# Attention and two gated layers on one core: another order for the first scores, their PSUM banks and the preparation of head pairs 1 and 2

## The chip, the cores and the metric

The kernel runs on one core of one Trainium2 chip. The metric is the device time of one execution in microseconds (us); lower is better. Before the change the median of three runs is 707.9 us (707.78 to 710.27).

## What is computed

Sixteen attention heads (2 batches of 8, 1152 positions, 64 columns) whose queries are averaged over pairs of positions, so that each head has 576 query rows against 1152 keys; then two gated layers on the 1152 by 512 result.

```python
q_pool = q.reshape(B, H, S // 2, 2, D).mean(axis=3)
scores = q_pool @ k.T / sqrt(D);  scores -= max(scores)
attn = exp(scores) / (sum(exp(scores)) + 1e-9);  o = attn @ v
x = o as (1152, 512)
xn = x / sqrt(mean(x*x) + 1e-6) * rms_g
x = (silu(xn @ w_gate) * (xn @ w_val)) @ w_out
out = (sigmoid(x @ w_gate2) * (x @ w_val2)) @ w_out2
```

## The kernel before, in words

The 16 heads are taken as 8 **pairs**; the two heads of a pair sit on partitions 0 to 63 and 64 to 127, so that two products of 64 rows run side by side on TensorE (PE). A pair's 576 query rows are cut into **chunks**: 1 to 4 of 128 rows, and chunk 0 with the last 64 rows of both heads. All products keep almost full precision: a tensor is split into a high part and a low part (`kh`, `kl` for keys, the two halves of `q` for queries), and each score is a sum of three products.

The work of a pair has these steps, and each has its helper:

- Raw Q, K and V come by DMA, issued by SyncE (SP) in program order (`load_q`, `load_k`, `load_v`, lines 307 to 327). GpSimd (POOL) adds the two positions of each query pair (`pool_q`, L333). It can only do so when raw Q has landed.
- PE turns pooled Q and raw K around (transposes, all of them on line 295, into tiles `qT` and `kT`), ScalarE (ACT) copies them out of PSUM (L359 to `kqt`) and POOL splits them (`prep_step` and `split`, L133 and L134). For pair 0 `prep_first` (L376 to L446) does this in pieces: K in three thirds, Q in chunks 1 and 2 first and 3, 4 and 0 later. There ACT writes the high part (L418), and VectorE (DVE, L421) or POOL (L425, from an ACT copy on L424) the low part.
- A **score unit** (`s_unit`, L448) is one chunk against one third of the keys (u = 0, 1, 2: 384 columns) for both heads: six matmuls of 384 columns on L467, into two PSUM banks with the tag "s", of which there are three. DVE takes the unit out of PSUM with its row maximum (`top`, L472, one per head; after the third unit of a chunk a small L474). Chunk 0 has its own three units on L464.
- When a chunk has all three units, ACT takes the exponentials (`expo`, L478, tile `e`).
- PE transposes the exponentials (`t_units`, tile `eT`, 24 or 30 of them on L295 in each cycle), into one of two double banks with the tag "t" that `qT` and `kT` use as well; ACT and DVE copy them to `et`.
- PE multiplies them by V (`av_unit`, L528, tile `o`, which has one bank of its own, tag "o"). Later steps turn the result into `x` and feed the gated layers (L683, L793, L822).

The order on each engine is written out by hand. An agenda (`at`, `run_agenda`, L119) holds steps with a slot g and a rank, and issues them in that order; each engine then runs its own queue in order and waits on semaphores. Eight slots are a cycle and six cycles are a pair (48 slots). `S_UNITS` says in which cycle and at which place of it a pair's units of chunks 1 to 4 stand, counted from the pair's first cycle; a cycle has two of them, and a pair's units begin five cycles ahead. `S_UNITS_SECOND` is pair 1's own table, which has three units in two of its cycles (cycles 3 and 4 of the program). `PREP` gives the cycles in which the next pair's Q, first five ninths of K and last four ninths of K are turned. Pair 0's first units start at slot -37.

The two lines that the units rest on are these:

```python
s = [bank("s", "s")[:, 0:SU] for j in heads]
for n, (x, ks) in enumerate(((0, kh), (0, kl), (1, kh))):
```

Of the kernel before, what the change touches and what calls it, by code (L numbers as in the profile page):

```python
# [27 lines left out]
S_UNITS_SECOND = ((-4, 1, 1, 0), (-3, 0, 1, 1), (-3, 1, 1, 2), (-3, 2, 2, 0), (-2, 0, 2, 1), (-2, 1, 2, 2), (-2, 2, 3, 0)) + S_UNITS[7:]  # L28
# [5 lines left out]
PREP = ((0, 1, 2), (-3, -2, 0))  # L34
# [17 lines left out]
def tile_attention_moe_moe(ctx, tc, q, k, v, w_gate1, w_val1, w_out1, rms_g, w_gate2, w_val2, w_out2, out):  # L52
# [315 lines left out]
    def prep_pair(c0, p):  # L368
        alloc_pair(p)
        slots = [(c0 + x) * CYCLE + PREP_SUB for x in PREP[p > 1]]  # L370
        at(slots[0], 1, lambda: prep_step(slots[0], q_group(p, (1, 2, 3, 4, 0), raw['s', p])))
# [4 lines left out]
    def prep_first():  # L376
# [64 lines left out]
        def turn():  # L441
            step(g0 + CYCLE + 1, q_group(0, (3, 4, 0), qs), True)

        at(g0 + 2, 21, rest)
# [423 lines left out]
```

## Time and profile before

| what | us |
|---|---|
| median of three runs | 707.9 |
| the profiled execution, its own time | 708.78 |
| its span, first to last instruction | 707.0 |
| PE busy in the span | 681.2 |
| DVE busy | 399.7 |
| ACT busy | 379.7 |
| POOL busy | 294.1 |

The span is what the profile shows of an execution; the execution's own time is 1.8 us more. Times in the rows are counted from the start of the span. The attention ends at about 253 us; the gated layers follow. PE counts as busy from the start of a matmul to its modelled end.

### The profile page before, as it was taken

How to read it: one execution, taken by the hardware profiler on the slowest of the kernel's cores; microseconds unless marked ns; L12 is line 12 of the kernel's file. 1: busy time of each engine (PE TensorE's matmuls, PEld its weight loads, DVE VectorE, ACT ScalarE, POOL GpSimd, SP SyncE). 2: the span in 40 equal slices, each digit the busy share in tenths (PEclk: the TensorE clock that was granted, in tenths of full speed). 3: DMA queues.
4: the chain of work that ended last, by engine and by line, in shares of the span. 5: the costliest groups of instructions: out<-in, count | busy, mean ns of one | idle time of the engine just before them, and what ended most of it. 6: DMA issues, size and time to landing. Idle time of an engine off the chain costs nothing.

```text
span 707.0 us, 13681 instructions
## 1 busy us (share of the span) xinstructions
PE 681.2 (96%) x5420; PEld 603.9 (85%) x5420; DVE 399.7 (57%) x1020; ACT 379.7 (54%) x708; POOL 294.1 (42%) x280
## 2 busy tenths in 40 slices
PE   7989999998989789999999999999999999999997
PEld 5767777776666489999999999999999999998886
DVE  4777887886886456886676533332546544642010
ACT  3768798797876436655454453324454545544000
POOL 3533364457431105663354374414434534537000
PEclk9999999999999999999999999999999999999999
DMA  6323314313111003332331243213113222222011
GB/s 183 112 69 107 93 47 134 97 42 96 34 33 32 2 0 116 118 124 62 90 116 64 68 142 116 69 32 112 60 61 119 67 84 90 90 69 80 1 74 59
DMA packets 66783, 55.92 MB, mean 79 GB/s; under 512 B 20896, under 2 KB 61856, under 8 KB 66720
## 3 DMA queue, kind: packets, MB, share of 16 engines
q1 hardware_dynamic: 66720, 55.06, 25.7%
q8 instruction: 42, 0.69, 0.4%
q14 instruction: 21, 0.17, 0.1%
HBM read 52.69 MB, written 2.36 MB: 78 GB/s over the span
## 4 chain that ended last, share of the span: by engine, by line
PE 64%; DVE 0%; issue 0%
PE acc L683 42%; PE acc L793 11%; PE acc L822 10%; PE xT L610 0%; DVE xa L599 0%; DVE ob L832 0%
## 5 line engine op out<-in xcount | busy, mean ns | idle before, releaser
L683 PE MATMUL acc<-xh,w 128*128 128x384 f32 (+2 forms) x1184 | 296.4, 331 | 0.0
L683 PEld LDWEIGHTS acc<-xh,w 128*128 128x128 f32 x1184 | 212.7, 189 | 0.1
L683 PE MATMUL acc<-xl,w 128*128 128x384 f32 (+2 forms) x592 | 196.0, 331 | 0.0
L244 POOL TENSOR_TENSOR w<-wr,w 128x512 fp32r<-128x512 f32 x68 | 100.0, 1471 | 186.8 <-ACT w L243 169.3
L472 DVE TENSOR_SCALAR_CACHE_REDUCE e<-s 128x384 f32<-128x384 f32 x216 | 114.3, 552 | 41.1 <-PE s L467 29.9
L229 POOL TENSOR_TENSOR wr<-wsg,wr 128x512 uint32<-128x512 uint32 x72 | 93.7, 1301 | 50.8 <-DVE wsg L223 43.5
L683 PEld LDWEIGHTS acc<-xl,w 128*128 128x128 f32 x592 | 111.6, 189 | 0.0
L478 ACT ACTIVATE e<-e,m 128x1152 f32<-128x1152 f32 x72 | 90.7, 1261 | 5.7 <-DVE m L474 5.7
L467 PE MATMUL s<-kh,q 64*128 64x384 f32 x384 | 87.0, 400 | 6.0 <-DVE e L472 5.1
L694 ACT ACTIVATE sg<-acc 128x384 f32<-128x384 f32 (+2 forms) x74 | 35.7, 482 | 104.3 <-PE acc L683 104.2
L697 DVE TENSOR_TENSOR sg<-acc,sg 128x384 f32<-128x384 f32 (+2 forms) x74 | 40.5, 547 | 84.6 <-PE acc L683 78.5
L528 PE MATMUL o<-et,vraw 128*64 128x320 f32 (+1 forms) x576 | 81.1, 418 | 0.0
L223 DVE SCALAR_TENSOR_TENSOR wsg<-wg,wsg 128x512 uint32<-128x512 uint32 x72 | 77.0, 1069 | 2.3
L201 ACT ACTIVATE wg<-wraw 128x512 f32<-128x512 f32 x72 | 48.4, 673 | 47.7 <-DVE wsg L223 38.7
L793 PE MATMUL acc<-hh,w 128*128 128x384 f32 x288 | 73.2, 334 | 0.0
L528 PEld LDWEIGHTS o<-et,vraw 128*64 128x64 f32 x576 | 37.5, 138 | 30.7 <-issue 10.1
L514 ACT ACTIVATE et<-eT 128x512 f32<-128x512 f32 x96 | 52.0, 598 | 21.1 <-PE eT L295 20.5
L467 PEld LDWEIGHTS s<-kh,q 64*128 64x128 f32 x384 | 50.8, 202 | 14.5 <-DVE e L472 11.9
L219 DVE TENSOR_SCALAR wsg<-wg 128x512 uint32<-128x512 uint32 x72 | 41.3, 573 | 35.0 <-POOL wr L229 34.9
L295 PE MATMUL eT<-ident,e 64*128 64x64 f32 x1296 | 54.3, 226 | 5.3 <-DVE xl L629 3.7
L295 PEld LDWEIGHTS eT<-ident,e 64*128 64x128 f32 x1296 | 51.4, 141 | 9.2 <-DVE xl L629 4.4
L208 ACT ACTIVATE wr<-wraw 128x512 uint32<-128x512 uint32 x72 | 47.9, 666 | 9.5 <-POOL w L244 8.5
(97 smaller groups left out, 872.7 us busy)
## 6 DMA issues: line engine op xcount, KB each, us to landing
wraw<-in_moe_w_gate_dram SPq DMA_DIRECT2D x24, 512.0 KB, 3.5
wraw<-in_moe_w_val_dram SPq DMA_DIRECT2D x24, 512.0 KB, 3.5
wraw<-in_moe_w_out_dram SPq DMA_DIRECT2D x24, 512.0 KB, 3.5
vraw<-in_v_dram SPq DMA_DIRECT2D x16, 288.0 KB, 3.1
kraw<-in_k_dram SPq DMA_DIRECT2D x14, 288.0 KB, 4.7
qraw<-in_q_dram SPq DMA_DIRECT2D x14, 256.0 KB, 3.7
out_dram<-ob SPq DMA_DIRECT2D x9, 256.0 KB, 2.0
qraw<-in_q_dram SPq DMA_DIRECT2D x14, 64.0 KB, 3.7
```

Of the source, the lines that this page charges most:

```text
L223: nc.vector.scalar_tensor_tensor(x["s"], x["g"], 3, x["s"], op0=ALU.logical_shift_left, op1=ALU.bitwise_or)
L229: nc.gpsimd.tensor_tensor(x["r"], x["s"], x["r"], op=ALU.add)
L244: nc.gpsimd.tensor_tensor(t[:, 1], r, t[:, 0].bitcast(F32), op=ALU.subtract)
L295: nc.tensor.transpose(t[:, j, (x0 + x) * 64:(x0 + x + 1) * 64], rows[j][r, cols], ident[r, r])
L467: nc.tensor.matmul(s[j], qt[r, x, QOF[c]:QOF[c] + P], ks[r, kc], start=(n == 0), stop=(n == 2))
L472: nc.vector.tensor_scalar(etile[p, c, j][:, kc], s[j], 1.0, None, op0=ALU.mult, op1=ALU.max, accum_out=m[:, u:u + 1])
L478: nc.scalar.activation(e, e, AF.Exp, bias=emin[p, c, j][:, NSU:NSU + 1], scale=1.0, accum_out=both_sums[p][:, j, c:c + 1])
L514: op = nc.vector.tensor_copy if n in E_DVE[cyc % NCYC] else lambda d, x: nc.scalar.activation(d, x, AF.Copy)
L528: nc.tensor.matmul(o[r, 0:n], vsb[p][:, j, kc], et[:, j * n:(j + 1) * n], start=(kc == 0), stop=(kc == NK - 1))
L683: nc.tensor.matmul(acc[:, 0:nt], wt[:, ws, dc * P:(dc + 1) * P], xs[:, dc], start=(dc == 0 and n == 0), stop=(dc == NDM - 1 and n == 2))
L793: nc.tensor.matmul(acc[t][:, 0:NTT], w[:, ws, (fc % 4) * P:(fc % 4 + 1) * P], hs[fc][:, cs], start=(fc == 0 and n == 0), stop=(fc == NFC - ...
L822: nc.tensor.matmul(acc[r][:, 0:DM], hs[fc][:, r * P:(r + 1) * P], w[:, ws, :], start=(fc == 0 and n == 0), stop=(fc == NFC - 1 and n == 2))
```

## The change

- In every score unit the three products come as high key by high query, high key by low query, low key by high query; the low part of K is used last, not second.
- Pair 0's first nine units get a table of their own (`S_FIRST`, slots -11 to -1): the first thirds of chunks 1 and 2 come first, and each third of K is turned just ahead of the units that use it. Every other unit takes one "s" bank and the "o" bank instead of two "s" banks. The rest of the table, chunk 4 and chunk 0, keeps its slots.
- Pair 1's Q and the first part of its K are turned at slot 0, ahead of the unit at slot 0, and the rest of its K at slot 8 (before: 0, 8 and 16). Pair 2's are turned at 40, 48 and 56 (before: 24, 32 and 48). Pair 1's units start one cycle sooner, and no cycle has three of them. `pool_q` of pair 1 moves from slot -8 to -5 of the new count, that of pair 2 from 16 to 32.
- SP issues raw Q and K of pair 1 ahead of V of pair 0.

```diff
-S_UNITS_SECOND = ((-4, 1, 1, 0), (-3, 0, 1, 1), (-3, 1, 1, 2), (-3, 2, 2, 0), (-2, 0, 2, 1), (-2, 1, 2, 2), (-2, 2, 3, 0)) + S_UNITS[7:]
+S_UNITS_SECOND = ((-5, 1, 1, 0), (-4, 0, 2, 0), (-4, 1, 1, 1), (-3, 0, 1, 2), (-3, 1, 2, 1)) + S_UNITS[5:]
+FIRST = -12
+S_FIRST = ((1, 1, 0), (3, 2, 0), (4, 1, 1), (5, 1, 2), (6, 2, 1), (7, 2, 2), (9, 3, 0), (10, 3, 1), (11, 3, 2))
-PREP = ((0, 1, 2), (-3, -2, 0))
+PREP_SLOTS = (-3, -2, 0)
+PREP = ((0, 0, 8), (5 * CYCLE, 6 * CYCLE, 7 * CYCLE))
...
-        slots = [(c0 + x) * CYCLE + PREP_SUB for x in PREP[p > 1]]
+        slots = PREP[p - 1] if p < 3 else [(c0 + x) * CYCLE + PREP_SUB for x in PREP_SLOTS]
...
+        load_q(1)
+        load_k(1)
         load_v(0)
-        load_k(1)
-        load_q(1)
...
-        for n, g in enumerate((g0 + 1, g0 + 4)):
-            at(g, 3, lambda n=n, g=g: step(g, k_group(0, 3 * n + 3, 3 * n + 6, kr), n == 1))
+        for n, x in enumerate((2, 3)):
+            at(FIRST + x, 3, lambda n=n, g=FIRST + x: step(g, k_group(0, 3 * n + 3, 3 * n + 6, kr), n == 1))
...
-        at(g0 + 2, 21, rest)
-        at(g0 + CYCLE + 1, 3, turn)
-        at(g0 + 2 * CYCLE, 22, lambda: diagonal(0))
+        at(FIRST + 4, 21, rest)
+        at(FIRST + 6, 3, lambda: step(FIRST + 6, q_group(0, (3, 4, 0), qs), True))
+        at(FIRST + 9, 22, lambda: diagonal(0))
...
-    def s_unit(g, p, c, u):
+    def s_unit(g, p, c, u, tags="ss"):
...
-        s = [bank("s", "s")[:, 0:SU] for j in heads]
-        for n, (x, ks) in enumerate(((0, kh), (0, kl), (1, kh))):
+        s = [bank(tags[j], "s")[:, 0:SU] for j in heads]
+        for n, (x, ks) in enumerate(((0, kh), (1, kh), (0, kl))):
...
+        if p == 0:
+            for n, (x, c, u) in enumerate(S_FIRST):
+                at(FIRST + x, 2, lambda g=FIRST + x, c=c, u=u, n=n: s_unit(g, 0, c, u, ("ss", "so")[n % 2]))
+        for x, n, c, u in (S_UNITS[-3:], S_UNITS_SECOND)[p] if p < 2 else S_UNITS:
-            at((cyc0 + min(PREP[p > 0])) * CYCLE, 0, lambda cyc0=cyc0, p=p: prep_pair(cyc0, p + 1))
-            at((cyc0 + POOL_Q) * CYCLE if p else -CYCLE, 50, lambda p=p: pool_q(p + 1))
+            at(min(PREP[p]) if p < 2 else (cyc0 + min(PREP_SLOTS)) * CYCLE, 0, lambda cyc0=cyc0, p=p: prep_pair(cyc0, p + 1))
+            at((-5, 4 * CYCLE)[p] if p < 2 else (cyc0 + POOL_Q) * CYCLE, 50, lambda p=p: pool_q(p + 1))
```

What moves on the engines is read from the order of the two programs' instructions. First PE at its start, behind the first transposes of Q (`kT<-ident,first` turns a third of pair 0's K, `s<-kh,q` and `s<-kl,q` are the products of score units), before:

```order
L295 MATMUL kT<-ident,first 128x64 x6
L467 MATMUL s<-kh,q 128x384 x2
L467 MATMUL s<-kl,q 128x384 x2
L467 MATMUL s<-kh,q 128x384 x2
L295 MATMUL kT<-ident,first 128x64 x12
L467 MATMUL s<-kh,q 128x384 x2
L467 MATMUL s<-kl,q 128x384 x2
L467 MATMUL s<-kh,q 128x384 x4
```

and now:

```order
L298 MATMUL kT<-ident,first 128x64 x6
L466 MATMUL s<-kh,q 128x384 x4
L466 MATMUL s<-kl,q 128x384 x2
L298 MATMUL kT<-ident,first 128x64 x6
L466 MATMUL s<-kh,q 128x384 x4
L466 MATMUL s<-kl,q 128x384 x2
L298 MATMUL kT<-ident,first 128x64 x6
```

The last two thirds of K were turned together behind the first unit; now each stands behind one unit more, and the low part of K closes a unit instead of standing in its middle.

Second, PE where the first exponentials are transposed (`eT<-ident,e`; `qT<-ident,qsum` and `kT<-ident,kraw` turn Q and K of pair 1, and `s<-kh,qbd` begins chunk 0), before:

```order
L467 MATMUL s<-kh,q 128x384 x2
L295 MATMUL qT<-ident,qsum 128x64 x10
L467 MATMUL s<-kh,q 128x384 x2
L467 MATMUL s<-kl,q 128x384 x2
L467 MATMUL s<-kh,q 128x384 x2
L295 MATMUL eT<-ident,e 128x64 x24
```

and now:

```order
L466 MATMUL s<-kl,q 128x384 x2
L298 MATMUL qT<-ident,qsum 128x64 x10
L298 MATMUL kT<-ident,kraw 128x64 x10
L466 MATMUL s<-kh,q 128x384 x4
L466 MATMUL s<-kl,q 128x384 x2
L298 MATMUL eT<-ident,e 128x64 x24
```

Ten transposes of pair 1's K have come ahead of the unit before the first exponentials. In both programs ten score units of pair 0 (chunks 1 to 3 and the first third of chunk 4) stand ahead of the first `eT`.

Third, POOL at the same time (`kl<-kqt,kh` is the low part of the last third of K, `qsum<-first` pools pair 0's Q, `q<-kqt,q` its late low part, `qsum<-qraw` pools pair 1's Q), before:

```order
L414 TENSOR_TENSOR qsum<-first 128x2x64 x3
L414 TENSOR_TENSOR qsum<-first 128x64 x2
L425 TENSOR_TENSOR kl<-kqt,kh 128x384
L425 TENSOR_TENSOR q<-kqt,q 128x384
L366 COPY qbd<-q 64x2x64 x2
L333 TENSOR_TENSOR qsum<-qraw 128x2x5x64
```

and now:

```order
L417 TENSOR_TENSOR qsum<-first 128x2x64
L428 TENSOR_TENSOR kl<-kqt,kh 128x384
L417 TENSOR_TENSOR qsum<-first 128x2x64 x2
L417 TENSOR_TENSOR qsum<-first 128x64 x2
L428 TENSOR_TENSOR q<-kqt,q 128x384
L336 TENSOR_TENSOR qsum<-qraw 128x2x5x64
```

The low part of the last third of K has come ahead of the late sums of Q, and pair 1's pooling ahead of the copies of `qbd`.

## Rows read from the trace of the kernel before

**Rows 1.** The page's first part: busy time, share of the span, instructions.
```profile
PE 681.2 (96%) x5420; PEld 603.9 (85%) x5420; DVE 399.7 (57%) x1020; ACT 379.7 (54%) x708; POOL 294.1 (42%) x280
```
**Rows 2.** Busy time in three stretches: length, engines, granted clock, DMA share, GB/s.
```profile
0.00:24.00 24.00, 17.98 (x105) 13.15 (x107) 12.10 (x48) 9.72 (x17) 7.90 (x20) 1.00 0.69 190
24.00:48.00 24.00, 21.48 (x284) 16.35 (x282) 17.38 (x66) 18.39 (x32) 12.64 (x14) 1.00 0.28 77
48.00:100.00 52.00, 51.85 (x706) 37.84 (x704) 40.51 (x158) 42.02 (x77) 22.95 (x30) 1.00 0.31 83
```
**Rows 3.** Timeline, one turn of the score loop: start, length, engine, [idle before <-releaser].
```profile
17.73 0.56 DVE L472 TENSOR_SCALAR_CACHE_REDUCE e<-s 128x384 f32<-128x384 f32 x1 [0.63 <-PE s L467]
18.21 0.08 DVE L472 DVE_READ_ACCUMULATOR e<-s 128x1 f32 x1
18.33 0.16 DVE L474 TENSOR_REDUCE m<-m 128x1 f32<-128x3 f32 x1
18.35 0.69 PE L467 MATMUL s<-kh,q 64*128 64x384 f32 x1 [0.35 <-DVE e L472]
18.40 0.55 DVE L472 TENSOR_SCALAR_CACHE_REDUCE e<-s 128x384 f32<-128x384 f32 x1
...
19.43 0.56 DVE L472 TENSOR_SCALAR_CACHE_REDUCE e<-s 128x384 f32<-128x384 f32 x1 [0.28 <-PE s L467]
```
**Rows 4.** Timeline of the head: low parts, first maximum, late low part of Q.
```profile
6.94 0.69 PE L467 MATMUL s<-kl,q 64*128 64x384 f32 x2
...
8.83 0.62 DVE L421 SCALAR_TENSOR_TENSOR kl<-kT,kh 128x192 fp32r<-128x192 f32 x2 [1.95 <-ACT kh L418]
...
9.37 0.55 DVE L472 TENSOR_SCALAR_CACHE_REDUCE e<-s 128x384 f32<-128x384 f32 x1
...
10.45 1.01 POOL L425 TENSOR_TENSOR kl<-kqt,kh 128x384 fp32r<-128x384 f32 x1
...
14.29 1.01 POOL L425 TENSOR_TENSOR q<-kqt,q 128x384 fp32r<-128x384 f32 x1 [2.83 <-ACT kqt L424]
```
**Rows 5.** Timeline where the first transposes and the tenth unit's maximum stand.
```profile
24.20 1.48 PE L295 MATMUL eT<-ident,e 64*128 64x64 f32 x21
...
24.55 0.56 DVE L472 TENSOR_SCALAR_CACHE_REDUCE e<-s 128x384 f32<-128x384 f32 x1 [0.35 <-PE s L467]
```
**Rows 6.** Timeline of ACT: the first of the exponentials.
```profile
14.10 1.26 ACT L478 ACTIVATE e<-e,m 128x1152 f32<-128x1152 f32 x1
```
**Rows 7.** Timeline: the first issue behind pair 0's Q, and pair 1's pooling.
```profile
8.44 1.06 SPq L327 DMA_DIRECT2D vraw<-in_v_dram  x2
...
18.51 1.55 POOL L333 TENSOR_TENSOR qsum<-qraw 128x640 f32<-128x640 f32 x1 [2.52 <-DVE m L474]
```
**Rows 8.** DMA issues between 8 and 20 us: count, KB each, median us to landing.
```profile
kraw<-in_k_dram SPq DMA_DIRECT2D x2, 288.0 KB, 4.8
qraw<-in_q_dram SPq DMA_DIRECT2D x2, 256.0 KB, 4.1
```
**Rows 9.** Timeline of PE's waits in pair 0's cycles 2, 3 and 4.
```profile
35.77 0.39 PEld L295 LDWEIGHTS qT<-ident,qsum 64*128 64x128 f32 x10 [0.39 <-POOL kl L134]
...
39.89 0.44 PE L467 MATMUL s<-kh,q 64*128 64x384 f32 x1 [1.09 <-DVE e L472]
...
46.07 0.44 PE L467 MATMUL s<-kh,q 64*128 64x384 f32 x1 [1.09 <-DVE e L472]
```
**Rows 10.** Timeline of PE: chunk 0 of pairs 0, 1 and 2 begins.
```profile
26.72 0.45 PE L464 MATMUL s<-kh,qbd 128*128 128x384 f32 x1
...
56.94 0.44 PE L464 MATMUL s<-kh,qbd 128*128 128x384 f32 x1
...
83.17 0.44 PE L464 MATMUL s<-kh,qbd 128*128 128x384 f32 x1
```
**Rows 11.** Matmuls of one line, 0 to 24 and 60 to 100 us: ns min/median/max.
```profile
L467 PE MATMUL s<-kh,q x39: 518/518/687, 6.3 to 23.9; 64*128 64x384 f32 x39
...
L467 PE MATMUL s<-kh,q x76: 328/376/443, 60.1 to 99.1; 64*128 64x384 f32 x76
```

More of the change, by code (lines that the diff above doesn't have):

```diff
@@ L429, in prep_first @@
             nc.tensor.transpose(warm[:, 0:P], ident, ident)
-        g0 = -4 * CYCLE - 5
         sums(slice(1, 3), (nc.vector, nc.gpsimd))
-        step(g0, q_group(0, (1, 2), qs), False)
-        step(g0, k_group(0, 0, 3, kr), False)
-        for n, g in enumerate((g0 + 1, g0 + 4)):
-            at(g, 3, lambda n=n, g=g: step(g, k_group(0, 3 * n + 3, 3 * n + 6, kr), n == 1))
+        step(FIRST, q_group(0, (1, 2), qs), False)
+        step(FIRST, k_group(0, 0, 3, kr), False)
+        for n, x in enumerate((2, 3)):
+            at(FIRST + x, 3, lambda n=n, g=FIRST + x: step(g, k_group(0, 3 * n + 3, 3 * n + 6, kr), n == 1))
         def rest():
@@ L439, in rest @@
                 sums(c, (nc.gpsimd, nc.gpsimd))
-        def turn():
-            step(g0 + CYCLE + 1, q_group(0, (3, 4, 0), qs), True)
-        at(g0 + 2, 21, rest)
-        at(g0 + CYCLE + 1, 3, turn)
-        at(g0 + 2 * CYCLE, 22, lambda: diagonal(0))
-    def s_unit(g, p, c, u):
+        at(FIRST + 4, 21, rest)
+        at(FIRST + 6, 3, lambda: step(FIRST + 6, q_group(0, (3, 4, 0), qs), True))
+        at(FIRST + 9, 22, lambda: diagonal(0))
+    def s_unit(g, p, c, u, tags="ss"):
         if p not in both_sums:
@@ L484, in s_unit @@
         for n, j in enumerate(heads):
-            at(g + (2 * n if g % CYCLE == S_SUB[0] else 0), 17 + n if c else 10, lambda j=j: top(j))
+            at(g + (2 * n if g % CYCLE == S_SUB[0] and g >= 0 else 0), 17 + n if c else 10, lambda j=j: top(j))
         if u == NSU - 1:
@@ L649, in tile_attention_moe_moe @@
         cyc0 = p * NCYC
-        for x, n, c, u in S_UNITS_SECOND if p == 1 else S_UNITS:
+        if p == 0:
+            for n, (x, c, u) in enumerate(S_FIRST):
+                at(FIRST + x, 2, lambda g=FIRST + x, c=c, u=u, n=n: s_unit(g, 0, c, u, ("ss", "so")[n % 2]))
+        for x, n, c, u in (S_UNITS[-3:], S_UNITS_SECOND)[p] if p < 2 else S_UNITS:
             g = (cyc0 + x) * CYCLE + S_SUB[n]
```

## The prediction

> **What bounds the kernel now.** I read the busy times first. PE is busy 96% of the span, no other engine above 57% [rows 1]. Then three stretches: PE is busy 18.0 of the first 24 us, 21.5 of the next 24 and 51.9 of the 52 behind them [rows 2]. So from 48 us on PE is the bound, and what the change can win lies ahead of that. Chunk 0 of pairs 0, 1 and 2 begins at 26.72, 56.94 and 83.17 [rows 10]: a pair costs 30.22 us the first time and 26.23 the second, when PE has no gap. Whatever is saved ahead of 57 us moves the dense rest to the left whole, since PE's queue is in order and its later work is the same.
>
> In the head the loop of the score units is the bound. A unit takes two of three "s" banks, so the next unit's second head must wait for the first maximum of this one: the maximum starts at 17.73, PE goes on at 18.35 having idled 0.35, and the next unit's maximum starts at 19.43 [rows 3]. From 9.37 to 24.55 there are nine such turns [rows 4, 5]: 15.2 / 9 = 1.69 us each. DVE and PE both idle in each turn.
>
> TensorE's clock matters here. The same matmuls last 518 ns in the head and 328 at the least later [rows 11]. The granted clock reads 1.00 for both stretches [rows 2], but these durations say that the head runs at the lower level, 1.2 GHz, and the rest at 2.4.
>
> **The change, part by part.** An edit with no cost: the new order of the three products has the same six matmuls and weight loads, so beyond the head it is worth 0; PE's density there [rows 2] leaves nothing to hide or lose.
>
> *The pace of the first units.* With "o" as a fourth bank two units are in flight and no unit waits for its neighbour. The bound becomes DVE: a maximum every 0.48 us (17.73 to 18.21), 0.19 more when a reduction follows (18.21 to 18.40) [rows 3]; a chunk is six of the first and two of the second, 3.26 us, so 1.09 per unit. PE is no slower: from its start at 18.35 to the next maximum at 19.43 is 1.08 us, latency included [rows 3].
>
> *The start.* The first unit ended with low queries by high keys; now it ends with the low keys, which PE multiplied from 6.94 for 0.69 us [rows 4], so the first maximum can start at 7.6 instead of 9.37. The 0.62 us of DVE work for the second third's low part [rows 4] stood ahead of it and now stands behind the first unit. The tenth unit's maximum can so start at 7.6 + 0.62 + 9 x 1.09 = 18.0 at the earliest. Before it was 24.55 [rows 5]; the upper end is 6.5 us.
>
> *New waits in the head.* (a) The low part of the last third of K is POOL's, 1.01 us [rows 4], behind ACT's two copies; walking the queues from unit to unit I have it ready at 11.1, and unit 4 then leaves DVE idle 0.6. (b) POOL makes pair 0's late sums of Q behind that and not ahead; their low part, another 1.01 us [rows 4], is ready at 15.0 and unit 7 needs it as its second product: 0.7. (c) Ten transposes of Q and ten of K of pair 1 stand ahead of unit 10. At 1.48 / 21 = 0.07 us [rows 5] they are 1.4, of which some 0.4 lie under DVE's remaining maxima: 1.0. Sum 2.3 us, so unit 10's maximum starts at about 20.3. Bounds: nothing (each input a little sooner) to 4 us (both POOL steps late by one more 1.01, and none of the transposes hidden). I take **4.3 us** won here, with ends of 2.5 and 6.5. ACT is late next: its late copies of Q end at about 13.9, where the four exponentials of 1.26 us [rows 6] begin, and a copy follows, so the first transposes can't start before 19.7; I have them at 20.0 (before 24.20).
>
> *The loads.* Raw Q of pair 1 takes V's place at 8.44 [rows 7]. With four issues of about 0.6 us and 4.1 to land [rows 8] it is there at 15.0, when POOL is free; POOL's 1.55 us end at 16.6 and PE asks at 18. Before it was pooled from 18.51 [rows 7]. Raw K is issued by 12.1 and there at 16.9 [rows 8]. V comes last, by 18.5, for a product at 26. All of it is hidden, with a reserve of over a us.
>
> *K of pair 1.* Ten transposes leave the place behind chunk 0, where the clock is up: half of 0.7 us, so **0.3** back (0 to 0.7).
>
> *Units of pair 1.* Two cycles with three units made PE wait 1.09 us each for a bank, behind DVE [rows 9]. With two units in every cycle, as in the dense pairs, this goes: **2.2 us** (0, if another wait takes its place, to 2.2).
>
> *Q and K of pair 2.* Q's transposes waited 0.39 us for POOL [rows 9]; two cycles later POOL is done: **0.4** (0 to 0.4). In exchange the last part of its K is turned only one cycle ahead of its first use, and a maximum of pair 1 now takes a tile that pair 0's third cycle still reads. Nothing in the trace shows either. They can cost 0, or as much as the nearest waits, 1.09 [rows 9]; each has most of a cycle to hide in, so I take **0.3 lost** for both.
>
> The sum is 4.3 + 0.3 + 2.2 + 0.4 - 0.3 = 6.9 us. A check from the other side: the first pair is 30.22 - 26.23 = 4.0 us longer than the second [rows 10], and the parts outside the head take 2.6 of these. The profiled execution (708.78, span 707.0) so becomes 701.9; it stands 0.9 above the median of 707.9, so the median becomes **701.0 us**.
>
> One rule of the skill speaks against part of this. In the trace the lower clock lasts through the head, and 26.72 already has a chunk-0 matmul of 0.45 us [rows 10]; the stretch before it mixed scores with 21 and more transposes [rows 5]. The Trainium skill (TensorE: Matmul & The Clock Gate, Part 4: PE-mode transpose) says that transposes do not count as PE being busy for the clock. By that rule the twenty transposes now set ahead of unit 10 would hold the clock down longer, and the sum would be the first rival's. No row here separates the two.
>
> **The rivals.**
>
> *The clock stays down until 26 us as before.* It rose at about 26 us, behind a stretch in which PE had no idle time. If it rises no sooner, what is done from 20.0 to 26.3 in the new order runs at 518 where 328 is possible [rows 11]: 6.3 x (1 - 328/518) = 2.3 us, some of it under DVE and ACT, say 2.0: **703.0**. For it: transposes are many there. Against: PE idled 0.35 of each 1.69 [rows 3] and has far less idle time from 8 us on in the new head.
>
> *Only the head gains.* ACT and POOL reach cycles 1 to 4 with less reserve, and new waits take the place of the 2.6 us outside the head: **703.6**. For it: ACT is busy 18.4 of 24 us behind the head [rows 2], and its four exponentials now run without a pause. Against: the later pairs do the same work in 26.2 us without a gap.
>
> *The change doesn't do what it says.* In the order of instructions the first transposes of exponentials stand behind ten units in both programs, so I count nothing for an earlier place. If the fourth bank also fails to quicken the loop, nine turns stay at 1.69: 7.6 + 0.6 + 15.2 = 23.4, a gain of 1.1 in the head and 3.7 in all: **704.2**. Against: the idle time in rows 3 is a wait for a bank and nothing else.
>
> *Slower than before: raw K of pair 1 comes late.* Its transposes now stand in front of unit 10 and of all of pair 0's exponentials, and PE is in order. Each us that K lands behind 18.5 is lost whole, and the gain of 6.9 is gone when it lands behind 25.4. Landing would take 13 us, not 4.8 [rows 8]; at three times 4.8 it is there at 26.5 and the kernel takes **709.0**. For it: the DMA engines are 69% busy in the head [rows 2]. Against: the bytes are the same as before.
>
> **How the numbers follow.** The forecast has a chance of 0.55; its own range, from the ends above, is 699.3 to 702.7. The clock rival has 0.13, the head alone 0.18, the unchanged pace 0.05, the late K 0.05; 0.04 is left for a head at its upper end of 6.5, 698.8. The range 699.0 to 704.6 leaves out the late K, the upper end and the worse third of two rivals, some 0.16. A measurement of this kernel tells about 0.5% from no change, 3.5 us, so faster means below 704.4: nearly all of the forecast (0.54) and the upper end (0.04), most of the clock rival (0.11), a little over half of the head alone (0.10), half of the unchanged pace (0.02): 0.81. Slower by over 0.5% takes a late K beyond its price, 0.03; 0.16 is left.
>
> **What would show it.** Right: unit 10's maximum near 20.3, a loop of about 1.1 us, the first exponentials' transposes at 20, chunk 0 of pair 1 near 50 and of pair 2 26.2 later, and no waits of 1.09 for a bank. The head alone is right if chunk 0 of pair 0 comes over 4 us sooner but that of pair 1 not over 5. The clock rival shows in 518 ns matmuls behind 20 us. The forecast is wrong if the loop stays at 1.69, or if PE waits for `kraw`, for POOL's low parts beyond 1.5 us, or for ACT's exponentials.

## The result, and the profile after

The changed kernel takes 699.89 us, the median of three runs (699.56 to 700.81), against 707.9. The ratio is 0.988 with a 95% interval of 0.985 to 0.991. The forecast was 701.0, so the gain is 8.0 us where 6.9 were expected. The profiled execution of the changed kernel is also 699.89 (span 698.1), against 708.78 (span 707.0).

The busy line of its page, and three windows (columns as in [rows 1, 2]):

```profile
PE 675.8 (97%) x5420; PEld 598.9 (86%) x5420; DVE 399.0 (57%) x1020; ACT 379.8 (54%) x708; POOL 294.0 (42%) x280
```

```profile
0.00:24.00 24.00, 19.09 (x171) 14.36 (x173) 16.01 (x65) 14.38 (x25) 12.00 (x24) 1.00 0.78 213
24.00:48.00 24.00, 23.92 (x328) 16.87 (x325) 18.86 (x74) 19.45 (x35) 9.55 (x14) 1.00 0.22 55
48.00:100.00 52.00, 51.84 (x714) 38.05 (x713) 42.62 (x164) 43.70 (x81) 27.06 (x33) 1.00 0.34 93
```

The second window, where PE was busy 21.48 us [rows 2], is now dense, and DVE does 16.01 us of work in the first one instead of 12.10. Behind 48 us little is different.

DVE's timeline in the head (start, length, engine, line, operation, idle time before it and its releaser): the first maximum, the two places where it then has to wait, and the tenth unit's maximum.

```profile
7.57 0.56 DVE L471 TENSOR_SCALAR_CACHE_REDUCE e<-s 128x384 f32<-128x384 f32 x1 [0.78 <-PE s L466]
...
11.77 0.56 DVE L471 TENSOR_SCALAR_CACHE_REDUCE e<-s 128x384 f32<-128x384 f32 x1 [0.69 <-PE s L466]
...
15.65 0.56 DVE L471 TENSOR_SCALAR_CACHE_REDUCE e<-s 128x384 f32<-128x384 f32 x1 [0.17 <-PE s L466]
...
18.94 0.56 DVE L471 TENSOR_SCALAR_CACHE_REDUCE e<-s 128x384 f32<-128x384 f32 x1
```

Nine turns with a wait in each [rows 3] have become a DVE that works through with 0.86 us of waits in all. The tenth unit's maximum starts at 18.94 instead of 24.55 [rows 5].

PE's timeline: two low-key products of the head, its two waits for POOL from which DVE's come, the first transposes of pair 1, the first of the exponentials, and chunk 0 of pairs 0, 1 and 2.

```profile
8.40 0.53 PE L466 MATMUL s<-kl,q 64*128 64x384 f32 x2
...
9.67 0.34 PE L466 MATMUL s<-kl,q 64*128 64x384 f32 x2
...
11.29 0.45 PE L466 MATMUL s<-kl,q 64*128 64x384 f32 x2 [0.52 <-POOL kl L428]
...
15.00 0.44 PE L466 MATMUL s<-kh,q 64*128 64x384 f32 x2 [0.37 <-POOL q L428]
...
17.21 0.50 PE L298 MATMUL qT<-ident,qsum 64*128 64x64 f32 x8
...
19.45 1.05 PE L298 MATMUL eT<-ident,e 64*128 64x64 f32 x24 [0.48 <-ACT kqt L362]
...
21.01 0.62 PE L463 MATMUL s<-kh,qbd 128*128 128x384 f32 x2
...
47.75 0.62 PE L463 MATMUL s<-kh,qbd 128*128 128x384 f32 x2
...
74.10 0.62 PE L463 MATMUL s<-kh,qbd 128*128 128x384 f32 x2
```

Against [rows 10], chunk 0 of pair 0 begins 5.71 us sooner (21.01 for 26.72), that of pair 1 9.19 sooner, that of pair 2 9.07 sooner, and the span ends 8.9 sooner. So the head won 5.71 and pair 0 another 3.48 (it lasts 26.74 instead of 30.22); from there on the two programs take the same time within 0.3 us. The rows at 8.40 and 9.67 are the same kind of pair of matmuls: 0.53 us, then 0.34. TensorE goes from its lower level (1.2 GHz) to the upper (2.4 GHz) at about 9.5 us. In the kernel before it did so at about 26: its transposes of exponentials at 24.20 are still long [rows 5].

### The profile page after: what moved, and what is told of

The parts are those of the page before. It is cut to its first block, busy times and chain, and to the rows that moved or that the text cites. A ratio compares the mean times of both kernels' runs of the same rounds, so it can differ in the third digit from the quotient of the medians.

```text
span 698.1 us, 13688 instructions
## 1 busy us (share of the span) xinstructions
PE 675.8 (97%) x5420; PEld 598.9 (86%) x5420; DVE 399.0 (57%) x1020; ACT 379.8 (54%) x708; POOL 294.0 (42%) x280
## 4 chain that ended last, share of the span: by engine, by line
PE 64%; DVE 0%; issue 0%
PE acc L685 43%; PE acc L795 11%; PE acc L824 11%; PE xT L609 0%; DVE xa L598 0%; DVE ob L834 0%
## 5 line engine op out<-in xcount | busy, mean ns | idle before, releaser
L466 PE MATMUL s<-kh,q 64*128 64x384 f32 x384 | 66.5, 387 | 1.5 <-ACT kh L421 0.6
L795 PEld LDWEIGHTS acc<-hh,w 128*128 128x128 f32 x288 | 52.1, 188 | 0.0
```

The source lines that it names most:

```text
L466: nc.tensor.matmul(s[j], qt[r, x, QOF[c]:QOF[c] + P], ks[r, kc], start=(n == 0), stop=(n == 2))
L795: nc.tensor.matmul(acc[t][:, 0:NTT], w[:, ws, (fc % 4) * P:(fc % 4 + 1) * P], hs[fc][:, cs], start=(fc == 0 and n == 0), stop=(fc == NFC - ...
```

## The experiments

Two things were to be found out: which parts of the change the 9 us come from, and why the head won 5.7 where 4.3 were forecast. The points in the trace by which the runs are compared, in us:

| run | median | first unit on PE | first max | tenth unit's max | first `eT` | chunk 0, pair 0 | pair 1 | pair 2 |
|---|---|---|---|---|---|---|---|---|
| before | 707.9 | 6.28 | 9.37 | 24.55 | 24.20 | 26.72 | 56.94 | 83.17 |
| after | 699.89 | 6.19 | 7.57 | 18.94 | 19.45 | 21.01 | 47.75 | 74.10 |
| after, three banks | 703.96 | 5.99 | 7.37 | 22.75 | 22.41 | 24.44 | 51.18 | 77.55 |
| before, fourth bank | 705.42 | 5.87 | 8.95 | 22.49 | 22.16 | 24.63 | 55.45 | 81.69 |
| after, old places for pairs 1 and 2 | 703.26 | 6.18 | 7.56 | 18.95 | 18.65 | 20.42 | 50.64 | 76.88 |
| after, old places for pair 2's Q and K | 700.46 | 6.06 | 7.44 | 18.81 | 19.32 | 20.89 | 48.22 | 74.46 |
| after, V first | 704.03 | 5.89 | 7.27 | 24.02 | 23.69 | 26.00 | 52.75 | 79.10 |
| after, old products | 700.19 | 6.06 | 7.75 | 19.02 | 19.64 | 21.20 | 47.93 | 74.29 |
| after, late queries sooner | 698.41 | 5.88 | 7.26 | 17.90 | 18.45 | 20.01 | 46.35 | 72.72 |

Two things limit these comparisons. The first unit starts on PE between 5.87 and 6.28, and the programs issue the same instructions ahead of it: how soon it can start depends on when raw Q and K of pair 0 land. So up to 0.4 us between two runs isn't the edit's, and where it matters the text also counts from the first unit's start; chunk 0 of pair 0 then comes 20.44 us later before the change and 14.82 after it. And beside the experiments the kernel before took 708.3 to 708.9, so that medians of different rows compare to about 1 us. The ratios are to these runs of before.

No run takes the order of the first units or of K's thirds away by itself, nor a line that the diff ahead leaves out, by which both maxima of a unit in the head are issued in the unit's own slot. They are in "everything else" below.

### The fourth bank: taken away, and alone

```diff
-                at(FIRST + x, 2, lambda g=FIRST + x, c=c, u=u, n=n: s_unit(g, 0, c, u, ("ss", "so")[n % 2]))
+                at(FIRST + x, 2, lambda g=FIRST + x, c=c, u=u, n=n: s_unit(g, 0, c, u, "ss"))
```

> The changed kernel with all of pair 0's first units in the three score banks, nothing else undone. Theory (the fourth bank takes the wait out of the loop): the loop of the units goes back to 1.5 to 1.7 us, the tenth unit's maximum starts at 22 to 23.5 us, not 18.9, and the kernel takes 703.5 to 704.5 us. Rival A (the order of the first units and of the loads makes the gain): the loop stays near 1.1 us, 700 us. Rival B (the clock makes the gain): the clock still rises near 9.5 us, the loop is about 1.3 us, the tenth maximum is at 20 to 20.5 and the kernel takes 701 to 701.5.

Measured: 703.96 (703.22 to 704.52), ratio to before 0.993 (0.992 to 0.995). PE's timeline of this run:

```profile
11.96 0.33 PE L466 MATMUL s<-kh,q 64*128 64x384 f32 x1
...
15.79 1.03 PE L466 MATMUL s<-kh,q 64*128 64x384 f32 x3 [0.34 <-DVE e L471]
...
16.94 0.52 PE L466 MATMUL s<-kh,q 64*128 64x384 f32 x1
17.80 1.01 PE L466 MATMUL s<-kh,q 64*128 64x384 f32 x3 [0.34 <-DVE e L471]
```

The wait for DVE's first maximum is back, 0.34 us (0.35 in [rows 3]), and so are turns of about 1.7 us (DVE's maxima that close such waits start at 17.17, 18.85 and 20.52). Chunk 0 of pair 0 comes 3.43 us later than with four banks (3.63 counted from the first unit). The clock had risen (0.33 us for a matmul at 11.96) and had fallen again at 16.94 (0.52); it rose for good at 23.6. So the 3.43 hold the waits and also the lower clock that went with them; no run parts the two.

The other way round, the kernel before with the "o" bank for every other unit of its first nine and nothing else changed:

```diff
-    def s_unit(g, p, c, u):
+    def s_unit(g, p, c, u, tags="ss"):
...
-        s = [bank("s", "s")[:, 0:SU] for j in heads]
+        s = [bank(tags[j], "s")[:, 0:SU] for j in heads]
...
-        for x, n, c, u in S_UNITS_SECOND if p == 1 else S_UNITS:
+        for i, (x, n, c, u) in enumerate(S_UNITS_SECOND if p == 1 else S_UNITS):
...
-            at(g, 2, lambda g=g, p=p, c=c, u=u: s_unit(g, p, c, u))
+            tags = "so" if p == 0 and i < 9 and i % 2 else "ss"
+            at(g, 2, lambda g=g, p=p, c=c, u=u, tags=tags: s_unit(g, p, c, u, tags))
```

> The kernel before with one edit: of pair 0's first nine units every other one takes the o bank for its second head. Theory (the bank sets the loop, and the late pooling of pair 1 sets what can be had of it): the loop falls from 1.69 to about 1.1 us, the ninth unit is done near 18.5, but the transposes of pair 1's Q, which wait for the pooling that starts at 18.5, hold the tenth unit until about 20.5; its maximum is at 21 to 21.7, not 24.55, and the kernel takes 704.5 to 705.5. Rival A (the order of the units is needed as well): the loop stays above 1.4 us, 706.5 or more. Rival B (the bank alone gives the head's whole gain): the tenth maximum at 19 to 19.5 and 702.5.

Measured: 705.42 (703.84 to 707.21), ratio 0.995 (0.993 to 0.996). PE's timeline:

```profile
11.43 0.69 PE L467 MATMUL s<-kl,q 64*128 64x384 f32 x2 [0.71 <-POOL kl L425]
...
20.49 0.80 PE L295 MATMUL qT<-ident,qsum 64*128 64x64 f32 x10 [1.27 <-POOL qsum L333]
...
24.63 0.69 PE L464 MATMUL s<-kh,qbd 128*128 128x384 f32 x1
...
55.45 0.44 PE L464 MATMUL s<-kh,qbd 128*128 128x384 f32 x1
```

The bank alone wins 2.09 us at chunk 0 of pair 0; everything else alone won 2.28 there (24.44). Together they win 5.71, so 1.3 us exist only when both are there. Counted from the first unit these are 1.68, 1.99 and 5.62, which leaves 1.95 for both. With the bank alone PE soon stands before the next late thing: POOL's low part of K (0.71) and POOL's sums of pair 1's Q (1.27), both of which the changed kernel has put in another place or loads sooner. Behind that last wait its matmuls are back at the lower level (0.69 us at 24.63), and the tenth unit's maximum comes at 22.49, later than the 21 to 21.7 expected.

### The places of pairs 1 and 2

```diff
-S_UNITS_SECOND = ((-5, 1, 1, 0), (-4, 0, 2, 0), (-4, 1, 1, 1), (-3, 0, 1, 2), (-3, 1, 2, 1)) + S_UNITS[5:]
+S_UNITS_SECOND = ((-4, 1, 1, 0), (-3, 0, 1, 1), (-3, 1, 1, 2), (-3, 2, 2, 0), (-2, 0, 2, 1), (-2, 1, 2, 2), (-2, 2, 3, 0)) + S_UNITS[7:]
...
-PREP = ((0, 0, 8), (5 * CYCLE, 6 * CYCLE, 7 * CYCLE))
+PREP = ((0, 8, 16), (3 * CYCLE, 4 * CYCLE, 6 * CYCLE))
...
-            at((-5, 4 * CYCLE)[p] if p < 2 else (cyc0 + POOL_Q) * CYCLE, 50, lambda p=p: pool_q(p + 1))
+            at((-5, 2 * CYCLE)[p] if p < 2 else (cyc0 + POOL_Q) * CYCLE, 50, lambda p=p: pool_q(p + 1))
```

> The changed kernel with the old table of pair 1's units and the old slots for the preparation of pairs 1 and 2; the head's units, banks and loads stay. Theory (the two waits for a bank and the late preparation cost 3.5 us between chunk 0 of pair 0 and of pair 1): chunk 0 of pair 0 begins near 21 as now, that of pair 1 at 50.5 to 51.3, not 47.75, with two waits of about 1.1 us behind DVE, and the kernel takes 702.5 to 703.5. Rival (the waits moved because the head is sooner, and the table is worth nothing): chunk 0 of pair 1 within 0.5 us of 47.75, 700 us.

Measured: 703.26 (702.53 to 704.2), ratio 0.992 (0.991 to 0.994). PE's timeline:

```profile
20.42 0.62 PE L463 MATMUL s<-kh,qbd 128*128 128x384 f32 x2
...
27.03 0.46 PE L298 MATMUL eT<-ident,e 64*128 64x64 f32 x8 [0.31 <-ACT kqt L362]
33.58 0.61 PE L466 MATMUL s<-kh,q 64*128 64x384 f32 x3 [1.10 <-DVE e L471]
39.76 0.61 PE L466 MATMUL s<-kh,q 64*128 64x384 f32 x3 [1.11 <-DVE e L471]
50.64 0.61 PE L463 MATMUL s<-kh,qbd 128*128 128x384 f32 x2
```

Pair 0 lasts 50.64 - 20.42 = 30.22 us again, to the hundredth what it was before the change. The two waits behind the cycles with three units are there, 1.10 and 1.11 ([rows 9] had 1.09), and so is one of 0.31 for ACT's copy of the late part of pair 1's K. At the same time chunk 0 begins 0.59 sooner than in the changed kernel (20.42 for 21.01): ten transposes of pair 1's K are out of the head. So the places are worth 3.48 in pair 0 and cost 0.59 in the head, 2.89 together.

The part of it that belongs to pair 2's Q and K, by itself:

```diff
-PREP = ((0, 0, 8), (5 * CYCLE, 6 * CYCLE, 7 * CYCLE))
+PREP = ((0, 0, 8), (3 * CYCLE, 4 * CYCLE, 6 * CYCLE))
...
-            at((-5, 4 * CYCLE)[p] if p < 2 else (cyc0 + POOL_Q) * CYCLE, 50, lambda p=p: pool_q(p + 1))
+            at((-5, 2 * CYCLE)[p] if p < 2 else (cyc0 + POOL_Q) * CYCLE, 50, lambda p=p: pool_q(p + 1))
```

> The changed kernel with the old slots for pair 2's Q and K and its pooling (24, 32, 48, pooling at 16); pair 1's units and preparation stay as changed. Theory (the later preparation of pair 2 is worth a short wait for POOL): chunk 0 of pair 1 later by 0 to 0.6 us, 700 to 700.6. Rival (most of the 3.5 us between chunk 0 of pair 0 and of pair 1 comes from pair 2's preparation, not from the units per cycle): chunk 0 of pair 1 later by 1.5 us or more, 701.5 or more.

Measured: 700.46 (699.82 to 701.32), ratio 0.988 (0.987 to 0.990). PE's timeline:

```profile
35.52 0.53 PE L298 MATMUL kT<-ident,kraw 64*128 64x64 f32 x10 [0.84 <-DMA kraw<-in_k_dram]
...
48.22 0.62 PE L463 MATMUL s<-kh,qbd 128*128 128x384 f32 x2
```

Pair 0 takes 48.22 - 20.89 = 27.33 us, 0.59 more than with the new places. The old wait for POOL (0.39 in [rows 9]) isn't what comes back: everything ahead is sooner now, raw K of pair 2 is not, and PE waits 0.84 for its DMA. Neither of the two costs that the forecast feared from the new places shows: PE waits for nothing between 25 and 50 us in the changed kernel.

### The order of the loads

```diff
-        load_q(1)
-        load_k(1)
         load_v(0)
+        load_k(1)
+        load_q(1)
```

> The changed kernel with SP's old order of the first loads: V of pair 0, then raw K and raw Q of pair 1. Theory (the new order of the loads is needed, because pair 1's pooled Q now stands in front of the tenth unit): pooling of pair 1 starts at 18 to 18.5, not 14.9, PE waits for it 2 to 3 us ahead of the tenth unit, and the kernel takes 702 to 703. Rival (the loads are hidden either way, as I had priced them in the sum): no difference above 0.3 us, 700.

Measured: 704.03 (701.18 to 704.88), ratio 0.993 (0.990 to 0.995). POOL's and PE's timelines:

```profile
19.91 1.53 POOL L336 TENSOR_TENSOR qsum<-qraw 128x640 f32<-128x640 f32 x1 [5.26 <-DMA qraw<-in_q_dram]
...
21.50 0.80 PE L298 MATMUL qT<-ident,qsum 64*128 64x64 f32 x10 [4.26 <-POOL qsum L336]
...
26.00 0.44 PE L463 MATMUL s<-kh,qbd 128*128 128x384 f32 x1
```

Raw Q of pair 1 comes behind V and K, so POOL sums it at 19.91 instead of 14.89, and PE stands for 4.26 us; the whole later program moves by 4.99 (26.00 for 21.01). That nearly undoes the head. The expectation was 1 to 2 us too low. The runs lie far apart; the one of 701.18 had a mean granted clock of 0.995, the one of 704.88 only 0.989.

### The order of the products

```diff
-        for n, (x, ks) in enumerate(((0, kh), (1, kh), (0, kl))):
+        for n, (x, ks) in enumerate(((0, kh), (0, kl), (1, kh))):
```

> The changed kernel with the old order of the three products of a unit, the low part of K in the middle. Theory (worth nothing in the dense part, and little in the head, where only units 1 and 4 wait for a low part of K): the tenth maximum later by 0.2 to 0.5 us, the pairs behind it 26.2 to 26.3 us each as now, 700 to 700.5 us. Rival (the order saves weight loads or time in every unit): each pair longer by 0.2 us or more, over 701.5 us.

Measured: 700.19 (699.98 to 701.73), ratio 0.989 (0.987 to 0.991). DVE's timeline:

```profile
7.75 0.56 DVE L471 TENSOR_SCALAR_CACHE_REDUCE e<-s 128x384 f32<-128x384 f32 x1 [1.10 <-PE s L466]
```

The order is worth 0.2 us in the head (21.20 for 21.01; 0.3 counted from the first unit) and nothing behind it (53.09 us from there to chunk 0 of pair 2 in both). It also tells what made the first maximum sooner. The forecast gave that to the product that closes the unit, and named DVE's queue behind it. With the old order the maximum still starts at 7.75, not at 9.37. What held it in the kernel before was, by its rows, DVE's own queue: the low part of K's second third stood ahead of it and began at 8.83 [rows 4].

### A version that beats both

The two waits left in the changed head are for POOL: the low part of the last third of K (DVE's 0.69 at 11.77) and the low part of the late queries (0.17). This variant gives unit 4 a third of K that is ready and lets POOL sum the late queries sooner.

```diff
-S_FIRST = ((1, 1, 0), (3, 2, 0), (4, 1, 1), (5, 1, 2), (6, 2, 1), (7, 2, 2), (9, 3, 0), (10, 3, 1), (11, 3, 2))
+S_FIRST = ((1, 1, 0), (3, 2, 0), (4, 1, 1), (5, 2, 1), (6, 1, 2), (7, 2, 2), (9, 3, 0), (10, 3, 1), (11, 3, 2))
...
-        at(FIRST + 4, 21, rest)
-        at(FIRST + 6, 3, lambda: step(FIRST + 6, q_group(0, (3, 4, 0), qs), True))
+        at(FIRST + 2, 21, rest)
+        at(FIRST + 5, 3, lambda: step(FIRST + 5, q_group(0, (3, 4, 0), qs), True))
```

> A version meant to be better than the changed kernel: pair 0's late sums of Q go ahead of the low part of the last third of K on POOL, its late Q is turned behind the fourth unit, and the fourth and fifth units change places, so that the one that needs POOL's low part comes later. Theory (POOL's two low parts leave DVE idle 0.7 and 0.2 us, and then ACT's four exponentials end last): the maxima run without a gap, but the first transposes of exponentials come only 0.3 to 0.6 us sooner than 19.45, at 18.9 to 19.15, since ACT is the bound there; 699.3 to 699.6 us. Rival (POOL alone sets the head): 1 us or more sooner, below 699.

Measured: 698.41 (697.12 to 698.76), ratio 0.985 (0.984 to 0.987). PE's timeline:

```profile
18.45 1.05 PE L298 MATMUL eT<-ident,e 64*128 64x64 f32 x24 [0.52 <-ACT kqt L362]
20.01 0.62 PE L463 MATMUL s<-kh,qbd 128*128 128x384 f32 x2
...
46.35 0.61 PE L463 MATMUL s<-kh,qbd 128*128 128x384 f32 x2
```

Chunk 0 of pair 0 comes 1.00 us sooner than in the changed kernel (0.69 counted from the first unit), that of pair 1 1.40, and the medians differ by 1.5. The intervals of the two ratios overlap, but the points in the trace don't leave the order open. What stands ahead of the first `eT` is ACT as in the changed kernel: it copies pair 1's Q and K behind the four exponentials (0.52). The gain is larger than expected because ACT itself is free sooner. Its copies of the late Q no longer stand right ahead of the exponentials, which begin at 12.74 instead of 13.74. ACT's timeline:

```profile
12.74 1.26 ACT L477 ACTIVATE e<-e,m 128x1152 f32<-128x1152 f32 x1 [1.01 <-DVE m L473]
```

The profiled spans of the two differ by 2.9 us, more than the head and pair 0 explain. The rest lies at the end of the attention. Windows of the changed kernel, and then of the variant (the column behind the five engines is the granted clock):

```profile
230.00:235.00 5.00, 3.48 (x24) 2.55 (x26) 2.80 (x7) 0.94 (x3) 0.68 (x1) 0.64 0.00 0
235.00:240.00 5.00, 4.79 (x24) 1.96 (x20) 1.16 (x3) 0.48 (x3) 0.00 (x0) 0.68 0.02 3
```

```profile
230.00:235.00 5.00, 4.94 (x34) 2.88 (x36) 3.21 (x9) 1.26 (x3) 0.00 (x0) 0.66 0.01 3
235.00:240.00 5.00, 4.46 (x37) 3.20 (x34) 0.00 (x0) 2.31 (x4) 0.64 (x1) 1.00 0.00 0
```

In both, PE waits 3.6 us for DVE (until 231.52 in the changed kernel, until 230.06 in the variant), and its clock is down behind that wait, longer in the first than in the second. The same instructions, from there to the next transposes of `oT`, take 8.81 us in the first and 7.38 in the second. So 1.4 of the 2.9 us are the clock of these two executions and not the edit; the variant's other three took 698.27 to 698.76, its profiled one 697.12. The gain over the kernel before isn't touched by it. There the clock is down behind the same wait and again behind a later one of 2.48 us (granted 0.63 from 254 to 258 us), and from the end of the first wait to the end of the span it takes 466.55 us, the changed kernel 466.58.

### What raises the clock

The clock rose 16 us sooner in the changed head. The first guess was that PE's idle time in each turn of the old loop kept it down. The kernel before with one unused matmul behind each of its first nine units:

```diff
+        if p == 0 and c and c < 4:
+            fill = bank("o", "fill")
+            nc.tensor.matmul(fill[:, 0:SU], qbd[:, 0], kh[:, kc], start=True, stop=True)
```

> The kernel before with nine matmuls added that nothing uses: one of 384 columns from zeros into the o bank behind each of pair 0's first nine units, to fill PE's idle time while it waits for a score bank. Rival (the clock makes the head's gain): the clock rises between 9 and 16 us, score matmuls last 330 to 420 ns from there, the loop falls from 1.69 to about 1.3 us although there are still three banks, and the kernel takes 704.5 to 705.5. Theory in its pure form (banks alone; what PE's clock does is hidden): the loop stays within 0.1 us of 1.69 and the kernel within 1 us of 707.9, or it is slower by the added matmuls.

Measured: 711.88 (711.7 to 712.91), ratio 1.005 (1.003 to 1.006). PE's timeline, one turn:

```profile
12.53 0.69 PE L467 MATMUL s<-kh,q 64*128 64x384 f32 x2
13.02 0.52 PE L467 MATMUL s<-kl,q 64*128 64x384 f32 x2
13.34 0.52 PE L467 MATMUL s<-kh,q 64*128 64x384 f32 x2
13.79 0.69 PE L470 MATMUL fill<-kh,qbd 128*128 128x384 f32 x1
```

No idle time stands in PE's rows from 12 us on, and yet the matmuls stay at 0.52 until 27.6. The fillers only lengthen the turns (chunk 0 at 29.67), so this run is a miss: a PE without a gap in its rows isn't enough. It doesn't settle the guess either. A row is as long as the latency of its matmuls, and rows overlap: the starts of this turn (the next row begins at 14.40) lie 0.49, 0.32, 0.45 and 0.61 us apart, where 0.32 is possible. So PE may still have stood idle within rows.

Then three kernels in which small unused matmuls, from the program's start on, take the place of the eight warm-up transposes: the changed kernel, the kernel before and the variant, each with 36 of them.

```diff
-        for _ in range(8):
-            nc.tensor.transpose(warm[:, 0:P], ident, ident)
+        hot = ap.tile([P, P], F32R, tag="hot", bufs=1, name="hot")
+        nc.vector.tensor_copy(hot, ident)
+
+        def heat(n):
+            for _ in range(n):
+                nc.tensor.matmul(warm[:, 0:P], hot, hot, start=True, stop=True)
+
+        heat(22)
...
+        heat(6)
...
+        heat(8)
```

> The changed kernel; the eight warm-up transposes on TensorE become 36 small unused matmuls (128 columns): 22 from the start on, 6 behind the first transposes of Q, 8 behind those of K. They fill TensorE's idle time ahead of the first unit at 6.2 us. In the changed kernel the score matmuls fall from 0.53 to 0.34 us a pair at about 9.5 us. Theory (the clock is what the head won beyond the forecast): pairs of 0.34 us from the first unit on; first maximum 0.2 to 0.4 us sooner, chunk 0 of pair 0 0.3 to 0.7 us sooner (20.3 to 20.7), 699.2 to 699.6 us. Rival (the warm-up doesn't raise the clock, or the head is bound by the copies of the first K anyway): 699.9 within 0.3, chunk 0 at 21.0.

> The kernel before, with the same 36 unused matmuls in place of its warm-up transposes. Theory 1 (the clock was down in the old head only because it was never raised, and stays up in the loop with three banks): a turn of 1.69 us becomes some 1.3, since the second head's matmuls halve behind the bank's release; nine turns give 3.5 us, 704 to 705. Theory 2 (three banks make TensorE wait in every turn, and the clock doesn't stay up through such waits, as it fell again at 12.8 us in the run of the changed kernel with three banks): the first units at 0.34 us a pair, then back to 0.53; a gain of 0 to 0.8 us, 707 to 708.

> The variant with the late queries sooner, with the same 36 matmuls. Theory: as for the changed kernel, 0.3 to 0.7 us on top of that variant's 698.4: 697.7 to 698.1, chunk 0 of pair 0 at 19.3 to 19.7 (20.0 without). Rival: 698.4 within 0.3.

Measured: 704.88 (704.58 to 705.4), 712.51 (712.26 to 712.71) and 703.19 (701.59 to 704.0); the ratios to before are 0.995, 1.005 and 0.992. All three miss what was expected. PE's timeline of the changed kernel with the 36:

```profile
1.60 4.96 PE L436 MATMUL warm<-hot 128*128 128x128 f32 x22 [1.60 <-DVE hot L432]
6.49 0.48 PE L298 MATMUL qT<-ident,qsum 64*128 64x64 f32 x4
...
14.37 0.52 PE L474 MATMUL s<-kl,q 64*128 64x384 f32 x2
...
26.06 0.44 PE L471 MATMUL s<-kh,qbd 128*128 128x384 f32 x1
```

Each small matmul takes 4.96 / 22 = 0.225 us, more than was reckoned with, so Q's first transposes start at 6.49 instead of 4.19 and the first unit at 10.78 instead of 6.19. And 9 us of them and of ten transposes, with no wait of PE from 1.60 to the first unit, don't raise the clock: in the third unit a pair still takes 0.52 us at 14.37. In the kernel before, with the 36, the turns stay at 1.68 and the clock stays down until 30 us.

One thing of use came from this. In the changed kernel with the 36, the clock was at the lower level once more from 20.9 to 25, just where pair 1's transposes and the tenth unit stand. A window of it (the column behind the five engines is the granted clock), and DVE's timeline:

```profile
21.50:24.00 2.50, 2.50 (x30) 2.50 (x31) 2.02 (x10) 2.50 (x6) 0.14 (x1) 0.52 0.69 198
```

```profile
24.40 0.56 DVE L479 TENSOR_SCALAR_CACHE_REDUCE e<-s 128x384 f32<-128x384 f32 x1 [0.81 <-PE s L474]
```

Here the tenth unit's maximum waits 0.81 us for PE; in the changed kernel, at the upper level, it doesn't wait at all (18.94, above). From the first maximum it comes after 24.40 - 12.15 = 12.25 us, there after 11.37.

The last run uses nine unused matmuls as wide as a unit's, on the variant:

```diff
-        hot = ap.tile([P, P], F32R, tag="hot", bufs=1, name="hot")
+        hot = ap.tile([P, SU], F32R, tag="hot", bufs=1, name="hot")
...
-        heat(22)
+        heat(6)
...
-        heat(6)
+        heat(1)
...
-        heat(8)
+        heat(2)
```

> The variant with the late queries sooner; its eight warm-up transposes become nine unused matmuls of 384 columns, as wide as a unit's: 6 from about 2.0 us, 1 behind the first transposes of Q, 2 behind those of K. At 0.32 to 0.36 us each they end at about 4.1, ahead of Q's sums, and at 5.95, ahead of the first unit at 5.9 to 6.2, so that the head isn't moved as it was by 36 narrow ones at 0.22 us each. Theory (the upper clock comes after some us of wide products without a pause, whatever they compute): pairs at 0.34 us sooner than 9.5, in the first or second unit; chunk 0 of pair 0 at 19.4 to 19.8 (20.0 without), 697.8 to 698.2 us. Rival 1 (only what the units themselves do raises it): still about 3.5 us behind the first unit, chunk 0 at 20.0, 698.4 within 0.3. Rival 2 (each takes 0.45 us and the first transposes come late): the whole head moves by what they are late, and the end with it: 0.5 us give 698.9.

Measured: 699.28 (697.5 to 700.38), ratio 0.987 (0.985 to 0.989). PE's timeline:

```profile
2.08 2.29 PE L437 MATMUL warm<-hot 128*128 128x384 f32 x6 [2.08 <-DVE hot L433]
...
6.77 1.01 PE L475 MATMUL s<-kh,q 64*128 64x384 f32 x4
7.58 0.52 PE L475 MATMUL s<-kl,q 64*128 64x384 f32 x2
...
10.01 0.34 PE L475 MATMUL s<-kl,q 64*128 64x384 f32 x2
...
16.59 0.84 PE L475 MATMUL s<-kl,q 64*128 64x384 f32 x2
```

The matmuls behind K's first transposes hold the first unit until 6.77 (5.88 without them), and chunk 0 of pair 0 comes at 20.98 for 20.01. That is nearest to the second rival, though each takes 0.32 and Q's first transposes aren't late (4.30). The clock is up at 9.5, in the third unit as without them, and down again by 16.59; the tenth unit's maximum then waits 0.82 for PE. What raises the clock therefore stays open. Where it rose by 9.5 us and stayed up, the units came with four banks and a turned third of K between them. This last run has both as well and doesn't keep it, so they aren't enough.

## Why the prediction was right, and which terms were off

**The bound.** Right. What was saved ahead of pair 1 arrived at the end nearly whole: 9.19 us at its chunk 0, 8.9 at the end of the span. The failed warm-up says the same from the other side: chunk 0 of pair 0 5.05 us later, the median 5.0 longer.

**The pace and the start.** Right in size: 1.1 us a unit (11.37 less 0.86 of waits and 0.53 for the low part of K, by nine) for the 1.09 forecast, first maximum at 7.57 for 7.6. Of the two reasons given for the start, the first weighs little. Counted from the first unit the maximum comes after 3.09 us before the change, 1.69 with the old products and 1.38 now, so the closing product is 0.31 of the 1.71 and DVE's queue the rest.

**The new waits in the head.** This is the step of the sum that was mis-sized. Forecast were (a) 0.6, (b) 0.7 and (c) 1.0, together 2.3; DVE's timeline has 0.69, 0.17 and none, together 0.86, and the head won 5.6 at the tenth unit's maximum where 4.3 were forecast. For (b) POOL's part was as late as reckoned (PE waited 0.37 for it at 15.00), but DVE still had maxima in the other banks to do. For (c) the twenty transposes were priced at the lower clock. They ran at the upper one, and the two runs with unused matmuls in which they met the lower one had 0.81 and 0.82 us of wait there, close to the 1.0. At the first `eT` 4.75 of the 5.6 were left, since ACT's copies hold it (0.48): 19.45, where 20.0 was reckoned. That is in small a sign that the forecast had set for being wrong, PE waiting for ACT, and also a wait that its own walk along the queues had found. Then came what no term of the sum held: from there to chunk 0 the same work, without a wait of PE in either, took 1.56 us for 2.52 before (24.20 to 26.72). These 0.96 go with the clock (24 transposes in 1.05 us, where 21 took 1.48 [rows 5]) and make up the 5.71.

**The rule against it.** At 9.67 the matmuls are at the upper level, behind two units with six transposes after each, and they stay there through the twenty of pair 1 and the 24 of the exponentials. So the rival in which the clock stays down until 26 us (703.0) is out. The Trainium skill (TensorE: Matmul & The Clock Gate, Part 4: PE-mode transpose) says that transposes don't count as PE being busy in the same way as other matmuls, for the clock; the trace of the changed kernel doesn't show them holding it down in such a mixture, nor does it show that they help. Another of its sections fits better here: the Trainium skill (TensorE: Matmul & The Clock Gate, A second HAM failure mode: psum-queue depth-cycling) says that cycling through banks leaves PE short idle times between its groups, and that the clock swings between its levels. The run with three banks agrees, up at 11.96 and down at 16.94. The run with fillers doesn't separate such idle times from other causes, and in the last run the clock fell behind waits that the variant has without a fall.

**Outside the head.** 3.48 for the 2.6 forecast. The two waits behind three units were 1.10 and 1.11, as forecast (2.2). K's ten transposes cost the head 0.59. What they gave back in pair 0 no run takes alone; 3.48 less 2.21 for the two waits and 0.59 for pair 2 leaves 0.68, where 0.3 was forecast, and a wait of 0.31 for ACT's copy behind them is part of it. Pair 2's Q and K were worth 0.59; forecast were 0.4 less 0.3 for new waits. Those waits are not there. The 0.4 was priced as a wait for POOL, and what comes back with the old places is a wait for raw K, so it is luck that the 0.4 is near.

**The loads.** They are hidden, as forecast: POOL sums pair 1's Q at 14.89 for the 15.0 reckoned, and PE waits for no raw tile. But the forecast priced this as a risk only. It is a condition: without it the other parts lose 5.0 us.

**The rivals.** "Only the head gains" and "the change doesn't do what it says" are out by 3.48 us in pair 0 and by the pace. Raw K was not late.

**The sum.** 5.7 and 3.5 against 4.3 and 2.6. For the profiled execution that gives 8.9 for 6.9; the median moved by 8.0, since before the profiled execution stood 0.9 above the median and after at it. The two parts erred the same way, by 1.4 and 0.9, and the range held.

## What to carry to other kernels

Where two engines take turns over few buffers, look at the other users of the ring (a bank that lies idle in the head will do), and count all that the quickened loop will ask for next: here the bank alone won 2.1 us, all the rest alone 2.3, both 5.7. A load that is hidden in the new order may be what makes that order possible, so price its absence too. Price a step by the clock that the new stretch will have, with both levels as ends, and treat a warm-up as work in an in-order queue: what it delays arrives at the end whole.

## What the runs showed of the hardware

- Rows without a gap don't mean the upper clock. From 12 to 27.6 us in the run with fillers, and through 9 us of small matmuls at the start, TensorE stayed at the lower level. The profile's granted clock said 1.00 for the first 24 us of the run with fillers; only the durations (0.52 for a pair, 0.34 at the upper level) tell. Once the clock has risen and fallen again the column agrees with the durations: 0.50 from 16 to 22 us with three banks, from 21 to 25 with the fourth bank alone and from 22 to 25 with V first, 0.52 in the window shown for the changed kernel with the 36. In these traces its 1.00 is wrong only ahead of the first rise.
- Matmuls of 128 columns with a weight load each follow each other every 0.21 us at the lower level (22 take 4.96 us and 8 take 1.97: 14 more in 2.99), those of 384 columns every 0.32 (the six of the last run start at 2.08, at 2.56 and from there every 0.32). Three times the columns cost 1.5 times the time.
- The clock can fall behind short waits: in the last run it was down by 16.59, though the longest wait that PE's rows show ahead of that, from the first unit on, was 0.23 us; in the same program without the nine matmuls it stayed up with the same waits. Why is open.
